# The ramp of a fused attention and MLP kernel: the linear matrix's products one visit sooner, one reciprocal one visit later

## The chip, the cores and the metric

The kernel runs on one core of a Trainium2 chip. The metric is the device time of one execution in microseconds (us), as the median of a few runs. Engines are named as in the profile: PE (TensorE matmul), PEld (its weight load), DVE (VectorE), ACT (ScalarE), POOL (GpSimd), SP (SyncE, which issues the DMAs).

## The reference

The inputs are `x` (4 x 12480 x 128), 32 inducing points, and the weights of an MLP with 2048 hidden units. Two attention blocks come first, then the MLP with a leaky activation whose slope `alpha` differs for each hidden unit.

```python
def mab(q, kv):
    s = scale * (q @ kv.transpose(0, 2, 1))
    s = s - s.max(-1, keepdims=True)
    a = np.exp(s)
    a /= a.sum(-1, keepdims=True) + 1e-09
    return a @ kv
h = mab(I, x)                   # 32 rows for each of the 4 batches
x = mab(x, h).reshape(49920, 128)
h = x @ w_in
g = np.maximum(h, 0.0) + alpha * np.minimum(h, 0.0)
out = (g @ w_out).astype(np.float32)
```

## The kernel before

The leaky activation is split: `g = (1 - alpha) * relu(h) + alpha * h`. The first part needs the hidden units, with `w_out` scaled by `1 - alpha` (`W1`). The second part is linear, so it is one 128 x 128 matrix, `Amat`, the product of `w_in` and `w_out` scaled by `alpha` (`winT` and `AW`, 16 products of 128 x 128 added up). The rows `a` of the second attention have 32 weights each, and both uses of them go through the 32 rows `h`: `HW` is `h` times `w_in`, `HA` is `h` times `Amat`.

**Visits.** The rows of a batch are cut into groups of 16 tiles of 128 rows, a group into blocks of 4 tiles. A block takes 4 visits. A visit issues four products `hh` = `a` times `HW` (L808; they share PE, 32 rows each), four activations of 128 x 512 from PSUM into `gt` (L821 on ACT or L823 on DVE), and then the 16 products of the visit before into the block's sum `bp` (L834). So the group of rows with number (0, 0) takes visits 0 to 3, 4 to 7, 8 to 11 and 12 to 15, and the second rows, group (0, 1), begin at visit 16. The linear products `bp` += `a` times `HA` (L861) are made for two blocks at a time; the first such pair waits until visit 8, and block 0 is finished there.

**The order is written by hand.** The engines run the program in the order in which it is issued. `at(n, fn, ...)` puts a small step behind the products of visit n; steps of one visit run in the order in which they were put there. Steps of the ramp that matter here:

- POOL scales `w_out` (L977 for `W1`, L986 for `AW`), then takes the maximum off the second rows' scores (L726), sums the first rows' exponentials (`first_sum`, ending in L1154), sums the second rows' (`b_sum`, ending in L736), and multiplies the second rows by their reciprocal (`b_mul`, L757).
- `linear_product`: the 16 products into a bank of PSUM (L996) and the cast to `Amat` on DVE (L999).
- `a_lin`: four small products `Amat` times `hT` (L619) and the cast to `HA` on DVE (L621).
- `first_rec`: the first rows' reciprocal on DVE (L1167), which waits for POOL's first sum. The output of the first four blocks is multiplied by it (L880).
- `b_rec`: the second rows' reciprocal on DVE (L749), which waits for POOL's second sum. `b_mul` waits for it, and `b_turn` has SP issue the transpose of the product (L766), which visit 16 reads.
- The four casts of a part of the next batch's `x` on ACT (L347) in visits 4 to 6.

**The planner.** `Plan.choose` searches once, before anything is issued, over all visits. It knows the costs given with `at` (`"s"` a PE step with a bank of PSUM, `"v"` DVE, `"a"` ACT, in ns) and chooses for each visit which activations go to ACT and which to DVE, which of the 8 PSUM banks each product uses, and whether the DVE or ACT part of a step is done at once or put off until between the second and the third activation of the next visit (`plan.then`, `run_waiting`). A chain with `("!", 0)` is not put off. The planner has no times for POOL and for DMAs.

Of the kernel before, what the change touches and what calls it, by code (L numbers as in the profile page):

```python
# [30 lines left out]
def kernel(  # L31
# [254 lines left out]
    def new_state(b):  # L286
        st = State()
        st.b = b
        st.pieces = whole_pieces if b else first_pieces
        st.np = len(st.pieces)  # L290
        st.xT = xt_pool.tile([C, NT, P], bf16, name="xT", tag="xT")
        st.xn, st.xs, st.s1, st.e1T, st.e1, st.s1p, st.hp = {}, {}, {}, {}, {}, {}, {}
        st.e2, st.m2, st.den2, st.rc, st.rep = {}, {}, {}, {}, {}

        st.mx = sm_pool.tile([P, NX], f32, name="mx", tag="mx")
        st.rm = sm_pool.tile([P, NX], f32, name="rm", tag="rm")
        st.fac = sm_pool.tile([P, NX], f32, name="fac", tag="fac")
        st.da = sm_pool.tile([P, NX], f32, name="da", tag="da")
        st.ex = sm_pool.tile([P, NX], f32, name="ex", tag="ex")
        st.den = sm_pool.tile([P, 1], f32, name="den", tag="den")  # L300
        st.hs = h_pool.tile([P, C], f32, name="hs", tag="hs")
        eng = nc.gpsimd if b else nc.vector
        eng.memset(st.mx[:], HIGH)
        eng.memset(st.da[:], 0.0)
        return st
# [380 lines left out]
    def b_exp(e, n):  # L686
        def work():
            nc.scalar.activation(out=e[:, :n], in_=e[:, :n], func=EXP, scale=scale)  # L688

        plan.then(work)  # L690
# [219 lines left out]
    st = new_state(0)  # L910
# [286 lines left out]
    def at(n, fn, *args, cost=()):  # L1197


        todo.setdefault(max(n, 0), []).append((fn, args, cost))  # L1200
# [5 lines left out]
    at(2, first_rest_exp, H, H, cost=[("a", 560), ("!", 0)])  # L1206
    at(2, first_turn_dma)
    at(6, first_rec, cost=[("v", 160)])
    at(6, linear_product, cost=[("s", 900), ("v", 210), ("!", 0)])
    at(7, a_lin, st, cost=[("s", 260), ("v", 210)])  # L1210
    blocks[0].later = True

    def on(b, fn, *args):
# [2 lines left out]
    for b, s, nt in groups[1:]:  # L1216
        n = first[b, s]
        when = [n - 23, n - 19, n - 16, n - 14, n - 13, n - 11, n - 9, n - 6]
        if (b, s) == (0, 1):
            when = [1, 2, 3, 4, 5, 7, 8, 8]  # L1220
        if (b, s) == (0, 2):
            when[7] = n - 7
        at(when[0], on, b, b_scores, s, nt, cost=[("s", 25 * nt), ("f", 0)])
        at(when[1], on, b, b_max, s, nt, cost=[("v", 70 + 33 * nt)])
        at(when[2], on, b, b_less_pool, s, nt)
        at(
            when[3],
            lambda b=b, s=s, nt=nt: b_exp(states[b].e2[s], nt),
            cost=[("a", 100 + 27 * nt)],
        )  # L1230
        at(when[4], on, b, b_sum, s, nt)
        at(when[5], on, b, b_rec, s, nt, cost=[("v", 160)])
        at(when[6], on, b, b_mul, s, nt)
        at(when[7], on, b, b_turn, s, 0, nt)
# [13 lines left out]
    for b in range(B - 1):  # L1248
# [3 lines left out]
        for p, pc in enumerate(whole_pieces):  # L1252
# [16 lines left out]
            else:  # L1269
# [9 lines left out]
                cost=[("s", 215 if f else 85), ("v", 800 if f else 460)],  # L1279
# [19 lines left out]
    for n, (blk, i) in enumerate(visits):  # L1299
# [9 lines left out]
        cost = nt * Plan.FREE if both else 0  # L1309
# [55 lines left out]
```

## Time and profile before

| | |
|---|---|
| median of 3 runs | 594.98 us (593.67 to 595.17) |
| profiled execution | 593.7 us, its span 591.9 us |
| granted TensorE clock | 0.998 |
| PE, PEld | 99%, 75% of the span |
| DVE, ACT, POOL | 90%, 91%, 37% |
| chain that ended last | PE 91%, DMA 5%, POOL 2% |

The span runs from the first to the last instruction; the rest of an execution's time lies around it. Busy time of PE includes the time in which a product that has been taken up waits. A timeline line gives start and length in us, the engine, the line of the kernel, the operation, what is written from what, shapes and count; in brackets is the idle time of the engine before it and what ended it. Lines of SPq are DMA issues.

### The profile page before, as it was taken

What the parts mean: (1) busy time and instruction counts of PE and PEld (TensorE: products, weight loads), DVE (VectorE), ACT (ScalarE), POOL (GpSimd) and SP (SyncE); (2) the same over time, 40 slices, a digit from 0 to 9 for tenths busy, and PEclk for the clock granted to TensorE, in tenths of its full rate; (3) what the DMA queues carried; (4) which work ended last, traced back from release to release, by engine and by line L of the source; (5) the groups of instructions that cost most, each with busy time, mean ns of one, the idle gap of its engine ahead of it and who ended that gap; (6) DMA issues with size and microseconds to landing.
All of it is one profiled execution on the core that took longest, in us unless ns stands there. A gap on an engine that the chain in (4) does not pass through costs nothing.

```text
span 591.9 us, 23144 instructions
## 1 busy us (share of the span) xinstructions
PE 584.5 (99%) x9500; PEld 441.3 (75%) x9500; DVE 535.5 (90%) x978; ACT 537.3 (91%) x1086; POOL 216.6 (37%) x260
## 2 busy tenths in 40 slices
PE   9999999999999999999999999999999999999997
PEld 6667777777777777777777777777777777777776
DVE  5889999999999898999999899999999999989996
ACT  5698999999999999999999999999999998999986
POOL 3494633323326426313226256124034034144010
PEclk9999999999999999999999999999999999999999
DMA  8969999233187999631368999731321331532421
GB/s 338 265 180 167 250 207 225 62 90 91 38 237 161 209 193 211 127 82 60 86 151 180 190 249 207 144 100 38 92 72 55 92 75 53 119 81 61 91 69 47
DMA packets 122347, 80.56 MB, mean 136 GB/s; under 512 B 103760, under 2 KB 106112, under 8 KB 119168
## 3 DMA queue, kind: packets, MB, share of 16 engines
q1 hardware_dynamic: 122016, 78.99, 56.3%
q8 instruction: 74, 1.21, 0.9%
q14 instruction: 33, 0.27, 0.2%
q10 hardware_dynamic: 224, 0.09, 0.1%
HBM read 28.07 MB, written 25.56 MB: 91 GB/s over the span
## 4 chain that ended last, share of the span: by engine, by line
PE 91%; DMA 5%; POOL 2%; DVE 0%; issue 0%; DVEq 0%; SPq 0%; ACT 0%; POOLq 0%
PE bp L834 64%; PE hh L808 21%; DMA xs<-in_x_dram 3%; PE bp L861 2%; DMA w_out_f<-in_moe_w_out_dram 2%; PE hh L644 2%; PE hh L473 1%; PE hh L379 1%; DMA e<-e1T 1%; POOL W L977 1%; POOL AW L986 1%; POOL t L712 0%; DVE gt L823 0%; DVEq L1360 0%; DVE xn L349 0%
## 5 line engine op out<-in xcount | busy, mean ns | idle before, releaser
L821 ACT ACTIVATE gt<-hh 128x512 bf16<-128x512 f32 x854 | 454.8, 605 | 36.0 <-PE hh L808 30.9
L823 DVE TENSOR_SCALAR gt<-hh 128x512 bf16<-128x512 f32 x706 | 453.5, 684 | 23.8 <-PE hh L808 13.3
L834 PE MATMUL bp<-W,gt 128*128 128x128 bf16 x6240 | 417.3, 220 | 0.2 <-DVE gt L823 0.2
L834 PEld LDWEIGHTS <-gt 128*128 128x128 bf16 x6240 | 349.4, 98 | 84.9 <-issue 76.6
L808 PE MATMUL hh<-a,HW 32*128 32x512 bf16 (+2 forms) x1664 | 156.2, 371 | 0.5 <-ACT gt L821 0.5
L757 POOL TENSOR_TENSOR rep<-e,rc 128x2048 bf16<-128x2048 f32 (+1 forms) x24 | 84.5, 3520 | 23.9 <-DVE rc L749 23.5
L726 POOL TENSOR_TENSOR e<-e,smx 128x512 f32<-128x512 f32 (+1 forms) x24 | 24.6, 1025 | 156.4 <-ACT gt L821 89.6
L808 PEld LDWEIGHTS <-HW 32*128 32x128 bf16 x1664 | 40.6, 91 | 41.7 <-issue 5.6
L712 POOL TENSOR_TENSOR t<-e 128x256 f32<-128x256 f32 (+1 forms) x24 | 17.2, 717 | 139.8 <-ACT e L688 139.7
L887 ACT COPY ob<-bp 128x512 f32<-128x512 f32 (+1 forms) x62 | 36.3, 585 | 4.3 <-PE bp L834 1.4
L712 POOL TENSOR_TENSOR t<-t 128x128 f32<-128x128 f32 (+3 forms) x100 | 30.3, 303 | 7.8
L330 POOL CAST xn<-xs 128x2048 bf16<-128x2048 f32 x17 | 32.1, 1888 | 2.8 <-DMA xs<-in_x_dram 2.3
L889 DVE COPY ob<-bp 128x512 f32<-128x512 f32 x32 | 22.0, 687 | 6.0 <-PE bp L834 6.0
L861 PEld LDWEIGHTS <-a 32*128 32x128 bf16 x392 | 15.0, 93 | 6.3 <-issue 0.5
L393 DVE TENSOR_SCALAR_CACHE_REDUCE s<-hh 128x512 f32<-128x512 f32 (+2 forms) x29 | 18.0, 619 | 1.6 <-PE hh L379 1.6
L861 PE MATMUL bp<-HA,a 32*128 32x128 bf16 x392 | 19.1, 214 | 0.2 <-DVE HA L621 0.2
L418 ACT ACTIVATE e1T<-s,rm 128x512 bf16<-128x512 f32 (+1 forms) x25 | 17.9, 718 | 0.6 <-DVE rm L402 0.6
L721 DVE TENSOR_REDUCE smx<-e 128x16 f32<-128x512 f32 (+1 forms) x24 | 15.9, 662 | 0.0
L963 PE MATMUL bp<-blank 128*128 128x256 bf16 x78 | 14.0, 316 | 1.2 <-DVE blank L909 1.2
L688 ACT ACTIVATE e<-e 128x512 f32<-128x512 f32 (+1 forms) x24 | 15.0, 625 | 0.2 <-POOL e L726 0.2
L489 DVE SCALAR_TENSOR_TENSOR hs<-hs,fac,hh 128x128 f32<-128x128 f32 (+1 forms) x25 | 8.6, 344 | 6.4 <-PE hh L473 5.7
L702 ACT COPY e<-hh 128x512 f32<-128x512 f32 (+1 forms) x23 | 13.9, 606 | 0.2
(110 smaller groups left out, 203.7 us busy)
## 6 DMA issues: line engine op xcount, KB each, us to landing
out_dram<-ob SPq DMA_DIRECT2D x97, 256.0 KB, 2.7
xs<-in_x_dram SPq DMA_DIRECT2D x23, 1024.0 KB, 6.6
xs<-in_x_dram SPq DMA_DIRECT2D x2, 512.0 KB, 9.1
w_in_f<-in_moe_w_in_dram SPq DMA_DIRECT2D x1, 1024.0 KB, 4.8
a<-rep SPq DMA_TRANSPOSE x25, 4.7
xT<-xn SPq DMA_TRANSPOSE x18, 6.0
e<-e1T SPq DMA_TRANSPOSE x18, 3.8
xs_left<-in_x_dram SPq DMA_DIRECT2D x4, 64.0 KB, 5.2
```

Source lines behind the costliest of these rows:

```text
L330: nc.gpsimd.tensor_copy(out=st.xn[s][:], in_=xs[:])
L393: nc.vector.tensor_scalar(out=s1[:parts, :cols], in0=ps[:parts, :cols], scalar1=-scale, scalar2=None, op0=MULT, op1=MIN, accum_out=st.mx[: ...
L712: nc.gpsimd.tensor_tensor(out=t[:, :n], in0=src[:, :n, :w], in1=src[:, :n, w : 2 * w], op=ADD)
L726: nc.gpsimd.tensor_tensor(out=st.e2[s][:, :n], in0=st.e2[s][:, :n], in1=st.m2[s][:, :n].unsqueeze(2).broadcast_to([P, n, M]), op=SUB,)
L757: nc.gpsimd.tensor_tensor(out=rep[:, :n], in0=st.e2[s][:, :n].unsqueeze(2).broadcast_to([P, n, R, M]), in1=rc[:, :n].unsqueeze(2).unsqueez ...
L808: nc.tensor.matmul(hh[:, q * cols + w.start : q * cols + w.stop], HWs[b][rows, v * P : (v + 1) * P], a2[rows, t0 : t0 + nt, :].rearrange(" ...
L821: nc.scalar.activation(out=gt[:, :cols], in_=hh[:, :cols], func=RELU)
L823: nc.vector.tensor_relu(gt[:, :cols], hh[:, :cols])
L834: nc.tensor.matmul(blk.acc[:, t * C : (t + 1) * C], gt[:, (q * nt + t) * P : (q * nt + t + 1) * P], W1[:, k, :], start=(not blk.begun), st ...
L861: nc.tensor.matmul(blk.acc[w, t * C : (t + 1) * C], blk.a2[rows, blk.t0 + t, w], HAs[b][rows, :], start=(not blk.begun and t == 0), stop=F ...
L887: nc.scalar.copy(out=ob[:, :nt], in_=acc)
L889: nc.vector.tensor_copy(out=ob[:, :nt], in_=acc)
```

## The change

The 16 products of the linear matrix go from visit 6 to visit 5 and the small products that follow from them from visit 7 to visit 6, each with the cast behind it. The second rows' reciprocal goes from visit 7 to visit 8, where the multiplication that reads it and the transpose stand already. `first_rec` stays in visit 6, now ahead of the small products instead of ahead of the 16. Costs are unchanged, but the planner sees them in other visits.

```diff
     at(6, first_rec, cost=[("v", 160)])
-    at(6, linear_product, cost=[("s", 900), ("v", 210), ("!", 0)])
-    at(7, a_lin, st, cost=[("s", 260), ("v", 210)])
+    at(5, linear_product, cost=[("s", 900), ("v", 210), ("!", 0)])
+    at(6, a_lin, st, cost=[("s", 260), ("v", 210)])
...
         if (b, s) == (0, 1):
-            when = [1, 2, 3, 4, 5, 7, 8, 8]
+            when = [1, 2, 3, 4, 5, 8, 8, 8]
```

The list `when` holds the visits of `b_scores`, `b_max`, `b_less_pool`, `b_exp`, `b_sum`, `b_rec`, `b_mul` and `b_turn`, in this order.

## The prediction

> **What bounds the kernel now.** I read the page first, then PE's timeline from 34 to 58 us, then the same stretch of DVE, POOL and SP, and last the chain of waits. The page:
>
> ```profile
> span 591.9 us, 23144 instructions
> PE 584.5 (99%) x9500; PEld 441.3 (75%) x9500; DVE 535.5 (90%) x978; ACT 537.3 (91%) x1086; POOL 216.6 (37%) x260
> ```
>
> PE is the bound, so an edit is worth what it takes out of PE's order, or puts into it. PE's timeline around the change (start, length, then engine and line; L808 are the four products that open a visit, L834 the sixteen that close the one before, L996 the linear matrix's products, L619 its small products, L861 the linear products that need HA):
>
> ```profile
> 38.53 0.40 PE L808 MATMUL hh<-a,HW 32*128 32x512 bf16 x4
> 39.76 1.06 PE L996 MATMUL hh<-AW,winT 128*128 128x128 bf16 x16
> 40.75 0.39 PE L808 MATMUL hh<-a,HW 32*128 32x512 bf16 x4
> 42.07 0.24 PE L619 MATMUL hh<-Amat,hT 128*32 128x128 bf16 x4
> 42.24 0.77 PE L808 MATMUL hh<-a,HW 32*128 32x512 bf16 x4
> 43.24 0.40 PE L861 MATMUL bp<-HA,a 32*128 32x128 bf16 x8 [0.22 <-DVE HA L621]
> 44.57 0.70 PE L808 MATMUL hh<-a,HW 32*128 32x512 bf16 x4
> 49.47 0.38 PE L861 MATMUL bp<-HA,a 32*128 32x128 bf16 x8
> ```
>
> Counting the L808 groups from 30.02 us, visits 5 to 9 begin at 37.20, 38.53, 40.75, 42.24 and 44.57, visit 12 at 49.24 and visit 16 at 54.77. A plain visit lasts 1.33 (37.20 to 38.53), and one with linear products 1.55 (visit 12: 49.24 to 50.79). Visit 6 lasts 2.22, which is 1.33 and 0.89 for sixteen products: no wait. Visit 7 lasts 1.49, which is 1.33 and 0.16 for four small ones: no wait. Visit 8 lasts 2.33 where 1.55 would do, so 0.78 is waiting. It has two parts: its L808 group takes 0.77 against 0.39, so 0.38 goes on PSUM banks; and L861 begins 1.00 after the visit's start, against 0.23 in visit 12, so 0.77 in all, of which 0.39 is left for HA. Visit 9's L808 group takes 0.70 against 0.39: 0.31 more on a bank. In all 1.08 us. The engine behind these waits is DVE:
>
> ```profile
> 41.40 0.25 DVE L1167 RECIPROCAL rec<-den 128x16 f32<-128x16 f32 x1 [0.49 <-POOL den L1154]
> 41.57 0.23 DVE L999 CAST Amat<-hh 128x128 bf16<-128x128 f32 x1
> 41.72 1.27 DVE L823 TENSOR_SCALAR gt<-hh 128x512 bf16<-128x512 f32 x2
> 42.91 0.28 DVE L621 CAST HA<-hh 128x128 bf16<-128x128 f32 x1
> 44.05 0.25 DVE L749 RECIPROCAL rc<-den 128x16 f32<-128x16 f32 x1 [0.86 <-POOL den L736]
> 44.22 0.63 DVE L823 TENSOR_SCALAR gt<-hh 128x512 bf16<-128x512 f32 x1
> ```
>
> Amat is cast only at 41.57, because the first rows' reciprocal (L1167) stands ahead of it and waits for POOL's sum; HA follows behind two activations and ends at 43.19. The second rows' reciprocal (L749) then holds DVE for 0.86, and visit 8's one activation on DVE stands behind it until 44.22; that one ends at 44.85, and PE's group of 44.57 waits for its bank. What feeds both:
>
> ```profile
> 33.03 4.03 POOL L986 TENSOR_TENSOR AW<-w_out_f,alT 128x512 bf16<-128x512 f32 x4
> 43.81 0.20 POOL L736 TENSOR_SCALAR den<-t 128x16 f32<-128x16 f32 x1
> 44.44 3.61 POOL L757 TENSOR_TENSOR rep<-e,rc 128x2048 bf16<-128x2048 f32 x1 [0.42 <-issue]
> 48.07 1.78 SPq L766 DMA_TRANSPOSE a<-rep  x1
> ```
>
> **The change, part by part.** No instruction is added or removed.
>
> Sixteen products, one visit sooner. On PE they move from 39.76 to the end of visit 5, where its L834 group ends 0.90 after 37.53, at 38.43. What they read is there: AW is written by 37.06 and winT landed near 30.7 (issue 25.40, 5.3 to landing). The cover is 1.4 us; if the loads of w_out came later by more than that, every further us would stand on PE. Their 0.89 leaves visit 6 and enters visit 5: visit 6 then begins at 39.42 and visit 7 at 39.42 + 1.33 + 0.16 = 40.91, the four small products having moved too; visit 8 begins at 42.24 as now. So the moves alone are worth nothing. Amat's cast (0.15 to the next start) goes ahead of visit 6's activations and of L1167; DVE is free there at about 39.0, and the sums come at about 39.6. Nobody else waits for it.
>
> HA. Its cast now comes from visit 6's work, right behind L1167, at about 41.6 or, if the planner puts it off, between visit 7's activations, at most 42.5. Visit 8 wants it at 42.47. So the 0.39 at L861 goes: **-0.39**. L1167 itself keeps its place and its POOL sum (41.37), so DVE still cannot pass 41.4 before it does visit 7's activations.
>
> Banks in visits 7 and 8. The 0.38 of visit 8 ends with visit 7's activations on DVE (41.72 and later) and ACT (41.51 and later, behind casts of x). Both are held as before. The small products' bank is now taken in visit 6, so one more is free in visit 8; against that, visit 6's activations start 0.89 later and visit 7 follows them 1.49 rather than 2.22 after. Best case -0.38 (all of it gone); worst a further wait as large as visit 9's, +0.31. I take **0**, the middle of two rows, because the same activations have to be done in the same time.
>
> The reciprocal, one visit later. L749 now stands behind visit 8's activations, so the one of 44.22 can run at about 43.2, and its bank is free well before visit 9: **-0.31**. POOL's sum still comes at 44.01, so if the reciprocal stands right behind that activation it runs at 44.05 as now. Queued behind it on DVE are visit 9's activations, which are not ready before 44.4 anyway (0.40 after the L808 start). If DVE takes the two output multiplications first (L880, 44.76 for two, 1.27), the reciprocal comes 1.2 later. Behind it waits the whole line of the second rows: POOL's multiplication of 3.61, SP's transpose, 4.3 from issue to landing by the DMA view, and visit 16. On POOL the casts of x (L335, L330) and on SP their transposes would shift by the same 1.2. Now the rows land at 52.4 and are read at 54.77: 2.4 us of cover. With visit 16 sooner by 0.7 and the landing later by 1.2, 0.5 is left. Cost: 0; bounds 0 and the rival's price below.
>
> Sum: -0.39 + 0 - 0.31 = -0.70 us. PE is the bound to the end, so it reaches the end. The profiled execution of before took 593.7 with a span of 591.9, 1.8 around it; I expect a span of 591.2 and 593.0 for such an execution. The median of the three runs, 594.98, lies 1.28 above the profiled one; taken off it, the forecast is **594.3**.
>
> The idle column alone shows only 0.22 of this, because waiting L808 groups are booked as busy; by idle time the edit would give 0.2 and not 0.7. I take the spacing of starts, since a visit's length is what the end feels. [...]
>
> **The rivals.** *The wait only changes its owner.* ACT works from 38.95 to 44.57 without a gap, on an exponential, four casts of x and activations. If PE comes sooner, ACT's activations end last instead, and visits 8 and 9 keep most of their waits; only L861's idle 0.22 is won: 594.8. For it: ACT's full timeline and visit 8's last L808, which waits for an ACT activation. Against: DVE loses 1.35 of idle time (0.49 and 0.86), which is two activations.
>
> *The second rows come late: slower.* The place is L808 of visit 16. If the reciprocal stands behind both output multiplications (45.3), POOL ends at 48.9 and SP issues at 49.3; the transposes' landings in this trace go from 3.1 to 6.2 us, so the rows arrive at 52.4 to 55.5. Visit 16 comes at 54.1 (54.77 - 0.70). It decides from an issue-to-landing of 4.8 on, and at 6.2 costs 1.4: 595.7; if visit 9's activations behind the late reciprocal lose the 0.31 again, 596.0. Against: 4.3 was this transpose's own time, which would leave visit 16 without a wait.
>
> *The planner decides otherwise for the rest.* It searches once over all visits, so other costs in visits 5 to 8 can move activations between ACT and DVE and change banks anywhere. Waits of PE after 46 us, by the same reading of starts, sum to about 3 us; a shuffle could win or lose some 2: 593.0 to 597.0. Against: in the second and third batch the same waits return 138.08 us apart (an L834 group of 1.24 at 195.86 and at 333.94, followed each time by an L808 group of 0.47), so the planner falls back into one pattern.
>
> *The change does nothing*, if the planner puts off Amat or HA as far as before: 595.0. Amat cannot be put off by its cost list, so this is weak.
>
> **How the numbers follow.** 0.3% is 1.8 us, about what a measurement of this kernel can tell from no change. Chances: forecast 0.56; other owner 0.15; late rows 0.13; planner 0.14; nothing 0.02. Faster by over 0.3% (below 593.2): 0.02 from the planner and 0.02 from a full -1.08 met by the runs' spread (1.3 below the median to 0.2 above), 0.04. Slower (above 596.8): 0.05 from the planner, 0.02 from rows landing later than any here, 0.03 from the runs' spread, 0.10. Within: 0.86. Range: the best sum is 593.9, and half of the lower spread takes it to 593.2; upward it takes in the late rows (596.0) and the nearer half of the planner's case, to 596.2.
>
> **What would show it.** L996 at about 38.4, HA before 42.5, visit 8's L861 0.2 to 0.6 after its first L808 and not 1.0, visit 9's L808 group at 0.40, visit 9 beginning near 44.2 and visit 10 near 45.9, no wait at visit 16, and the rest of PE's order as before. Wrong if visit 8 still takes over 2.1, if L749 starts after 45, or if the waits of later visits differ by more than 1 us.

## The result

The change made the kernel slower: 597.02 us median of 8 runs (594.75 to 599.22) against 593.62 of 8 runs before (592.79 to 595.17), ratio 1.0055, 95% interval [1.004, 1.007]. The forecast was 594.3, a gain. The profiled execution took 596.9 us with a span of 595.1, 3.2 more than the span of before. The page of the changed kernel, with the row of the opening products of a visit, and below it that row of the kernel before:

```profile
span 595.1 us, 23143 instructions
...
PE 584.9 (98%) x9500; PEld 441.4 (74%) x9500; DVE 536.5 (90%) x979; ACT 537.3 (90%) x1085; POOL 216.7 (36%) x260
...
L808 PE MATMUL hh<-a,HW 32*128 32x512 bf16 (+2 forms) x1664 | 156.0, 371 | 3.3 <-DMA a<-rep 2.8
```

```profile
L808 PE MATMUL hh<-a,HW 32*128 32x512 bf16 (+2 forms) x1664 | 156.2, 371 | 0.5 <-ACT gt L821 0.5
```

The engines' work is the same to within 1.0 us (DVE has 536.5 for 535.5). What is new is in the last column: PE stood idle for 2.8 us in front of one L808 group, for a transpose of the rows `a`.

**The ramp did what was forecast.** PE's timeline of the changed kernel in the lines that answer to those of before:

```profile
38.80 1.06 PE L996 MATMUL hh<-AW,winT 128*128 128x128 bf16 x16
39.79 0.40 PE L808 MATMUL hh<-a,HW 32*128 32x512 bf16 x4
...
41.28 0.59 PE L808 MATMUL hh<-a,HW 32*128 32x512 bf16 x4
...
42.80 0.39 PE L808 MATMUL hh<-a,HW 32*128 32x512 bf16 x4
43.03 0.38 PE L861 MATMUL bp<-HA,a 32*128 32x128 bf16 x8
...
44.35 0.39 PE L808 MATMUL hh<-a,HW 32*128 32x512 bf16 x4
```

Visit 0 began 0.37 later in this execution (30.39 against 30.02), before anything that the edit moves. Visit 8 lasts 1.55 (42.80 to 44.35), without a wait: L861 begins 0.23 after it. Visit 9's group takes 0.39. Only visit 7 has a wait of 0.20 on a bank. From visit 0 to visit 16 PE needs 23.85 us, 0.89 less than before.

**The loss sits at one place, visit 32,** where the third rows, group (0, 2), are first read. PE there in the kernel before, then in the changed kernel, and below it the changed kernel's clock by stretches (us, PE busy, PEld, DVE, ACT, POOL, granted clock, DMA share, GB/s):

```profile
78.39 0.40 PE L808 MATMUL hh<-a,HW 32*128 32x512 bf16 x4
...
79.73 0.40 PE L808 MATMUL hh<-a,HW 32*128 32x512 bf16 x4
...
81.18 0.53 PE L808 MATMUL hh<-a,HW 32*128 32x512 bf16 x4
```

```profile
76.86 1.07 PE L834 MATMUL bp<-W,gt 128*128 128x128 bf16 x16
80.73 0.61 PE L808 MATMUL hh<-a,HW 32*128 32x512 bf16 x4 [2.80 <-DMA a<-rep]
81.28 1.89 PE L834 MATMUL bp<-W,gt 128*128 128x128 bf16 x16
83.09 0.61 PE L808 MATMUL hh<-a,HW 32*128 32x512 bf16 x4
83.64 1.15 PE L834 MATMUL bp<-W,gt 128*128 128x128 bf16 x16
```

```profile
78.00:80.00 2.00, 0.00 (x0) 0.00 (x0) 0.47 (x1) 0.59 (x2) 0.00 (x0) 1.00 1.33 91
80.00:82.00 2.00, 1.27 (x12) 0.84 (x13) 0.56 (x1) 0.54 (x2) 0.00 (x0) 0.61 0.97 276
82.00:84.00 2.00, 2.00 (x20) 1.37 (x19) 1.49 (x4) 0.96 (x4) 0.00 (x0) 0.54 0.92 313
84.00:86.00 2.00, 2.00 (x33) 1.50 (x31) 1.91 (x4) 2.00 (x5) 0.00 (x0) 1.00 1.23 260
```

Visit 32 was due at 77.87 (visit 31's start and 1.33) and began at 80.73. Behind the wait the granted clock is 0.61 and 0.54, the sixteen products take 1.89 instead of 1.07, and visits 32 and 33 together 4.00 instead of 2.79. The balance: +0.37 for the later start, -0.89 from the ramp, +2.87 for the wait, +1.21 for the clock, 3.56 in all at visit 34. The spans differ by 3.2; the rest is won back far later, 0.24 near 230 us and 0.09 near 524.

**How the rows came to be late.** DVE's lines in the changed kernel, then SP's issues of before, then those of the changed kernel:

```profile
41.55 0.28 DVE L621 CAST HA<-hh 128x128 bf16<-128x128 f32 x1
...
43.29 1.29 DVE L823 TENSOR_SCALAR gt<-hh 128x512 bf16<-128x512 f32 x2 [0.16 <-PE hh L808]
44.50 0.24 DVE L749 RECIPROCAL rc<-den 128x16 f32<-128x16 f32 x1
```

```profile
49.95 1.56 SPq L894 DMA_DIRECT2D out_dram<-ob  x2
51.61 1.17 SPq L356 DMA_TRANSPOSE xT<-xn_left  x1
52.88 3.13 SPq L356 DMA_TRANSPOSE xT<-xn  x1
56.06 0.57 SPq L315 DMA_DIRECT2D xs<-in_x_dram  x1
...
69.38 1.19 SPq L449 DMA_TRANSPOSE e<-e1T_left  x1
...
72.93 2.31 SPq L766 DMA_TRANSPOSE a<-rep  x1
```

```profile
50.39 1.58 SPq L894 DMA_DIRECT2D out_dram<-ob  x2
52.06 2.10 SPq L356 DMA_TRANSPOSE xT<-xn_left  x1
54.26 3.26 SPq L356 DMA_TRANSPOSE xT<-xn  x1
57.57 1.00 SPq L315 DMA_DIRECT2D xs<-in_x_dram  x1
...
66.52 4.12 SPq L356 DMA_TRANSPOSE xT<-xn  x1
70.73 2.11 SPq L449 DMA_TRANSPOSE e<-e1T_left  x1
...
74.87 2.95 SPq L766 DMA_TRANSPOSE a<-rep  x1
```

The reciprocal runs 0.45 later, behind two activations (0.37 is the later start of this execution), and so do the second rows and the two output stores behind them (50.39 against 49.95). From there 0.44 grows to 1.51 at the load of x (57.57 against 56.06) and to 1.94 at the third rows' transpose. The first store lands 4.87 us after its issue (55.26) and not 2.96 (52.91). The load lands at 64.54 instead of 62.54, POOL's cast of it waits 1.64, and the third rows' multiplication starts at 66.45 instead of 65.39. But that multiplication is done at 70.06, and SP comes to the transpose of its rows only at 74.87. SP issues one thing after the other, and ahead of it the transpose of x at 66.52 takes 4.12 where it took 3.00, and the one of e at 70.73 takes 2.11 where it took 1.19. The rows land at 80.68. In the kernel before they landed at 78.30 and were read at 78.39: they had 0.09 us of cover, which is the time from a transfer's landing to its first reader.

### The profile page after: what moved, and what is told of

The parts are those of the page before. It is cut to its first block, busy times and chain, and to the rows that moved or that the text cites. A ratio compares the mean times of both kernels' runs of the same rounds, so it can differ in the third digit from the quotient of the medians.

```text
span 595.1 us, 23143 instructions
## 1 busy us (share of the span) xinstructions
PE 584.9 (98%) x9500; PEld 441.4 (74%) x9500; DVE 536.5 (90%) x979; ACT 537.3 (90%) x1085; POOL 216.7 (36%) x260
## 3 DMA queue, kind: packets, MB, share of 16 engines
q8 instruction: 74, 1.21, 0.9%
## 4 chain that ended last, share of the span: by engine, by line
PE 95%; DMA 4%; DVE 0%; DVEq 0%; ACT 0%; issue 0%; POOL 0%; SPq 0%
PE bp L834 65%; PE hh L808 22%; DMA xs<-in_x_dram 3%; PE bp L861 2%; PE hh L644 2%; PE hh L473 1%; DMA a<-rep 1%; PE hh L379 1%; PE bp L963 1%; PE hh L364 0%; PE hh L598 0%; PE hh L456 0%; DVEq L1360 0%; DVE xn L349 0%; PE hh L582 0%; PE hh L521 0%
## 5 line engine op out<-in xcount | busy, mean ns | idle before, releaser
L808 PE MATMUL hh<-a,HW 32*128 32x512 bf16 (+2 forms) x1664 | 156.0, 371 | 3.3 <-DMA a<-rep 2.8
L808 PEld LDWEIGHTS <-HW 32*128 32x128 bf16 x1664 | 40.3, 91 | 44.5 <-issue 5.8
L861 PEld LDWEIGHTS <-a 32*128 32x128 bf16 x392 | 15.0, 93 | 5.8
L861 PE MATMUL bp<-HA,a 32*128 32x128 bf16 x392 | 19.1, 214 | 0.0
```

The costliest lines, as they stand in the source:

```text
L808: nc.tensor.matmul(hh[:, q * cols + w.start : q * cols + w.stop], HWs[b][rows, v * P : (v + 1) * P], a2[rows, t0 : t0 + nt, :].rearrange(" ...
L861: nc.tensor.matmul(blk.acc[w, t * C : (t + 1) * C], blk.a2[rows, blk.t0 + t, w], HAs[b][rows, :], start=(not blk.begun and t == 0), stop=F ...
```

## The experiments

Every kernel was timed in 5 rounds beside the kernel before, unless said otherwise. The theories: A, the reciprocal's 0.45 us grows by itself along SP's queue; B, PE merely comes sooner to rows that had no cover; C, the transfers and not SP's order set when the rows land; F, formed after the first four, a packet of 16 KB of the queue that the DMA view lists as `q8 instruction` runs into the output stores.

**The two parts apart.** `e1_products`, against the changed kernel:

```diff
-            when = [1, 2, 3, 4, 5, 8, 8, 8]
+            when = [1, 2, 3, 4, 5, 7, 8, 8]
```

> The changed kernel with the second rows' reciprocal put back to visit 7; the 16 products and the small ones stay one visit sooner. On DVE this differs from the changed kernel in one place (the reciprocal stands two activations further ahead), PE's and SP's orders are the same. Theory A (the reciprocal's 0.45 us on POOL grows on SP's queue into 2.4 us at the third rows' transpose): POOL's multiplication starts at about 44.4 again, the third rows land at about 78.3, visit 32 comes at about 77.9 and waits 0.4, the clock stays full: 593 us, 0.5 below before. Rival B (PE comes 0.9 sooner to a transpose that had 0.1 us of cover, and the transfers' lateness is no matter of the reciprocal): landing near 80.7 and a wait of 2.8 as in the changed kernel, 597 us.

Measured: 594.21 us, ratio 1.0006 [0.9997, 1.0015]. The first store took 2.91, as before, and the third rows' transpose was issued at 72.80 (72.93 before). PE was due at visit 32 at 77.80 instead of 78.39, and the transpose landed at 78.87 instead of 78.30:

```profile
78.92 0.39 PE L808 MATMUL hh<-a,HW 32*128 32x512 bf16 x4 [1.05 <-DMA a<-rep]
```

The granted clock stayed at 1.00 from 74 to 86 us. So B holds for about half of this wait, 0.59; the other half, 0.57, is the transpose, which took 6.07 to land for 5.37. Together they take back more than the 0.48 that PE won from visit 0 to 16 (24.26). They do not make 3 us.

`e2_recip`, on the kernel before, has this diff the other way round: 7 becomes 8.

> The kernel before with the reciprocal alone moved from visit 7 to visit 8. On DVE it only changes places with one activation. If the reciprocal is the cause (A in its simple form): POOL's multiplication 0.4 later and the third rows landing 2 us late, 596 us or more. If it costs nothing by itself, since DVE waits for POOL's sum until 44.05 in both orders: multiplication at 44.4 as before, visit 9 sooner by 0.31, visit 32 waiting 0.2 for rows that land at 78.3: 593.4 us, within 0.3 of before. Rival B: as this, since PE comes only 0.3 sooner.

Measured: 593.58 us, ratio 0.9994 [0.9985, 1.0003]; the rows landed at 77.86, visit 32 did not wait. The reciprocal ran right when POOL's sum was there (43.80), as the prediction had it for the whole change; so this run has no late reciprocal, and does not test A. Neither part alone loses anything that can be told; the two together lose 0.55%.

**Where the chain can be broken.** `e3_turn` and `e4_load`, each against the changed kernel:

```diff
-            when[7] = n - 7
+            when[7] = n - 8
```

> The changed kernel with the transpose of the third rows (L766 of group (0, 2)) issued one visit sooner, which puts it on SP ahead of one transpose of e (L449) and one output store. A and B: issue at about 72.9 instead of 74.9, landing near 78.7, the wait at visit 32 falls from 2.8 to about 0.9, and the clock is not lowered after it: 3.3 us off, about 593.7 us. Rival C (the transfers, not SP's order, set the landing): landing at 80.7 as before, 597 us. If the transpose of e that is pushed back is needed at once, PE waits for it at L473 instead.

```diff
-                    0: (-1, -1, 7), 1: (-1, 9, 10), 2: (4, 9, 11), 3: (12, 20, 21)
+                    0: (-1, -1, 7), 1: (-1, 9, 10), 2: (4, 9, 11), 3: (7, 20, 21)
```

> The changed kernel with the load of the fourth piece of the next batch's x (1 MB, L315) issued in visit 7 instead of visit 12, so that it runs at about 47 to 51 us, where the DMA engines are nearly idle, and not from 57.6 to 64.5. Theory A (a queue of transfers and of SP's issues that is full from 50 to 80 us): POOL's cast of that piece no longer waits for it (1.6 us in the changed kernel), the third rows' multiplication starts at about 64.9 instead of 66.5, the issues behind it come 1 to 2 us sooner, and the wait at visit 32 is under 0.5: about 592.7 us, below before. Rival B: the wait stays near 2.8, 597 us. Against both: the second rows' transpose runs beside the load and lands up to 1 us later, which visit 16's cover of 1.4 takes.

`e3_turn`: 594.70 us, ratio 1.0011 [1.0002, 1.002], 1.0 more than expected. The stores landed late again (55.09), but the transpose was issued at 72.35, landed at 78.61, and visit 32 waited 1.17 idle, with a granted clock of 1.00 over the span. SP's order is part of the chain, and C is out. A is out too: the reciprocal ran at 44.05 here, to the hundredth as in the kernel before, and the stores were late all the same. `e4_load`: 593.83 us, ratio 1.0007 [0.9998, 1.0016]. No wait at visit 32, as A had it; but the load held up the second rows' transpose, which landed at 54.76 (52.78 in the changed kernel), and visit 16 waited 0.98. The cover that I had given as 1.4 was smaller than the load's price, a miss.

**The packet and the stores.** Each trace has 74 packets of 16 KB in `q8 instruction`, in the median some 256 PE instructions apart (matrix products and weight loads, about 19000 in all). Set beside the first output store (times in us; "packet after" counts from the store's issue; the last column is visits 32 and 33 together):

| kernel | store issued, landed | took | packet | packet after | third rows landed | wait at visit 32 | two visits |
|---|---|---|---|---|---|---|---|
| before | 49.95, 52.91 | 2.96 | 53.48 | 3.5 | 78.30 | 0 | 2.79 |
| e1_products | 49.34, 52.25 | 2.91 | 52.72 | 3.4 | 78.87 | 1.12 | 2.77 |
| e2_recip | 49.70, 52.66 | 2.96 | 53.09 | 3.4 | 77.86 | 0 | 2.79 |
| changed | 50.39, 55.26 | 4.87 | 52.28 | 1.9 | 80.68 | 2.87 | 4.00 |
| changed, again | 50.09, 55.13 | 5.04 | 51.83 | 1.7 | 80.24 | 2.79 | 4.19 |
| e3_turn | 49.95, 55.09 | 5.14 | 51.86 | 1.9 | 78.61 | 1.23 | 2.77 |
| e12_filler | 50.03, 55.08 | 5.05 | 51.79 | 1.8 | 80.51 | filled | 2.65 |
| e5_wide | 49.74, 52.73 | 2.99 | 53.76 | 4.0 | 78.12 | 0.95 | 2.77 |
| e11_narrow | 49.32, 54.08 | 4.76 | 51.22 | 1.9 | 79.45 | 1.68 | 2.77 |

Where the packet starts 1.7 to 1.9 after the store's issue, the store takes 4.8 to 5.1; where it starts 3.4 or more after it, 2.9 to 3.0. Of the five traces not in the table four fall in the same groups (`e6_products_turn` 3.4 and 2.92, `e9_all` 4.0 and 2.94, `e10_before_wide` 6.9 and 2.97, `e7_load6` 1.9 and 5.09). `e4_load` does not: 1.0 and 3.68. The second store of the pair, issued some 1.2 behind the first, narrows the step: with the packet 2.22 to 2.26 behind its issue it took 4.2 (`e1_products`, `e2_recip`, `e6_products_turn`), with 2.35 it took 2.66 (the kernel before). `e8_again` is the changed kernel unaltered, run once (596.59 us):

> The changed kernel once more, for a second profile. Theory F: where the packet of the instruction queue comes while the stores run (before 53), stores land after 55 and visit 32 waits 2 to 3; where it comes after them, visit 32 waits under 1 and the time is near 594.5. Theory A: the stores land after 55 each time.

The packet was early, the stores landed after 55, visit 32 waited 2.79. And here visit 0 began when it did in the kernel before (30.03), the reciprocal ran at 44.13, 0.08 later than there, and the first store was issued 0.14 later. SP came to the third rows' transpose 1.10 later (74.03), and it landed 1.94 later. So the 0.45 of the first profile was not needed for the loss.

The last two lines of the table change the number of PE instructions ahead of visit 0. `e5_wide`, against the changed kernel:

```diff
-    blank = const.tile([P, 2 * P], bf16, name="blank")
+    blank = const.tile([P, 4 * P], bf16, name="blank")
...
-            nc.tensor.matmul(ps[:, : 2 * P], blank[:, :P], blank[:], start=True, stop=True)
+            nc.tensor.matmul(ps[:, :w], blank[:, :P], blank[:, :w], start=True, stop=True)
...
-        for _ in range(n):
+        for w in [4 * P] * (n // 2) + [2 * P] * (n % 2):
```

> The changed kernel with the warm-up products on a blank tile twice as wide and half as many (512 columns instead of 256): the same PE time, but 64 PE instructions fewer before visit 0, so that each later 16 KB packet of the instruction queue, which come some 256 PE instructions apart in all traces so far, comes about 2.1 us later (64 at the 30 instructions a us of a visit). Theory F (in the changed kernel that packet, at 52.3, meets the two output stores of 50.4 and 51.6 on one DMA engine; the stores land 2.3 late, and SP's transposes and loads behind them pass it on to visit 32): packet near 54.4, the first store lands near 53.2, the third rows near 78.5, the wait at visit 32 under 1, about 593.3 us. Theory A in its first form (0.45 us of delay on POOL and SP grow by themselves): stores land at 55.3, third rows at 80.7, 597 us.

Measured: 594.80 us, ratio 1.0012 [1.0000, 1.0024], against 1.0055 of the changed kernel. The store was on time, the load landed at 62.33, the rows at 78.12, and the granted clock over the span was 1.00. What is left at visit 32 is the products' wait, 0.95. The time is 1.5 above what was expected; the profile has one more wait, 1.49 in the middle of an L861 group at 361.69, that it puts down to nothing it shows. The edit also brought the load of `w_out` and POOL's work behind it forward (POOL's second sum ended at 42.97, in `e8_again` at 43.51), but the reciprocal stands behind DVE's activations there and came only 0.28 sooner. The control, `e10_before_wide`, is this edit on the kernel before:

> The kernel before with the wider warm-up products alone, a control for e5_wide. Theory F: in the kernel before the packet of the instruction queue came after the first store had landed, so 64 instructions fewer gain nothing there: ratio 1.000, 594 us. If wider warm-up products are themselves worth some 2 us (a higher clock early, a shorter start), the time falls to 592.

593.46 us, ratio 0.9997 [0.9983, 1.001]: by itself the edit is worth nothing. `e11_narrow` goes the other way on `e1_products`, the first 17 warm-up products of 256 columns made as 34 of 128:

```diff
-    def warm(n):
+    def warm(n, w=2 * P):
...
-    warm(17)
+    warm(34, P)
```

> The kernel with the products sooner alone (e1_products, 594.2 us, in which the packet at 52.7 came after the first store had landed at 52.3), with the first 17 warm-up products of 256 columns made as 34 of 128: the same PE time, 34 PE instructions more, so the packet comes about 1.1 us sooner, near 51.5, while the stores issued at 49.4 and 50.5 run. Theory F: the stores land near 54.7, the third rows near 80 and visit 32 waits over 2, with a lowered clock behind it: 596.5 us, with the reciprocal unmoved. If the reciprocal's move is needed for the loss: 594.2.

594.82 us, ratio 1.0019 [1.0008, 1.003], 0.6 above `e1_products` (the two intervals overlap). The packet came where it was meant to, the store took 4.76 with the reciprocal unmoved, the wait rose from 1.12 to 1.68. So the first store can be late without the reciprocal's move, with 34 PE instructions more far ahead and the packet 1.9 behind its issue instead of 3.4. But the size was a quarter of what I had expected, and it did not come down the queue: the third rows' transpose was issued at 72.88, in `e1_products` at 72.80. Nearly all of the 0.56 lies between its issue and its landing, 6.57 for 6.07. Here the stores had been 0.8 sooner than in `e8_again` to begin with, and the load landed at 62.60, before POOL was free for it.

That leaves a rival that was not tried: later packets could meet the third rows' transpose itself. In the eight traces in which a packet starts 2.7 to 5.0 us after the issue of this transpose, it lands after 5.8 to 6.6 us; in the other six, after 4.7 to 5.6. `e5_wide` and `e11_narrow` change the number of PE instructions ahead of these packets too. So it is shown that PE instructions more or fewer far ahead shift the first packet against the store and the store's time with it (4.76 for 2.91 in `e11_narrow`, 2.99 for 4.87 in `e5_wide`), and in the changed kernel the rows' landing too (78.12 for 80.68, `e5_wide`); how much of the rows' lateness comes by the stores and SP's queue, and how much by later packets, is not.

**The clock.** `e12_filler`, on the changed kernel, has 12 products of 512 columns behind visit 31, read by nobody:

```diff
+    at(31, filler, cost=[("s", 2600)])
```

> The changed kernel with 12 products of 512 columns that nobody reads (2.56 us) at the end of visit 31, in the time in which PE waits for the third rows. If the wait of 2.8 is all of the loss, this costs nothing and gains nothing: 597 us. If PE's lowered clock behind the idle wait costs the 1.3 that visits 32 and 33 take too long: the clock stays full, these two visits take 1.4 each, and the time falls by 1.3 to 595.7 us, although PE does more.

595.65 us, ratio 1.0024 [1.0009, 1.0039], and the two visits took 2.65. PE and the clock:

```profile
77.36 2.75 PE L1216 MATMUL hh<-W,blank 128*128 128x512 bf16 x12
80.56 0.39 PE L808 MATMUL hh<-a,HW 32*128 32x512 bf16 x4 [0.45 <-DMA a<-rep]
80.88 1.07 PE L834 MATMUL bp<-W,gt 128*128 128x128 bf16 x16
```

```profile
80.00:82.00 2.00, 1.55 (x25) 1.10 (x24) 0.88 (x2) 0.96 (x2) 0.00 (x0) 1.00 0.79 242
82.00:84.00 2.00, 2.00 (x33) 1.46 (x30) 1.96 (x4) 2.00 (x6) 0.00 (x0) 1.00 0.92 337
```

The rows were as late as ever (80.51). 2.75 us of work without use made the kernel some 1.4 faster: the granted clock behind it is 1.00 and not 0.61 and 0.54, and the two visits take 2.65 and not 4.00.

**Versions.** `e6_products_turn` is `e1_products` with the line of `e3_turn`; `e7_load6` is `e4_load` with 6 for 7; `e9_all` is `e5_wide` with the line of `e3_turn`.

> The kernel with the products sooner and the reciprocal where it was (e1_products), with the third rows' transpose issued one visit sooner, ahead of one transpose of e. There the wait at visit 32 was 1.1, with issue at 72.8 and landing at 78.9. All theories that blame the landing: issue near 70.9, landing near 76.5, no wait at visit 32: 1.1 less than e1_products, 593.1 us and about 0.15% under before. If the products' gain is lost for another reason, 594.2 as e1_products.

593.22 us, ratio 0.9987 [0.9979, 0.9996]: the rows landed at 75.47, visit 32 began at 77.69 with no wait. It beats both kernels, by 0.13% the one before.

> The changed kernel with the load of the fourth piece of x in visit 6 instead of 12: issued at about 39.7, ahead of the first transpose of x, which has 10 us to spare, and not directly ahead of the second rows' transpose, which e4_load made 2.4 late (visit 16 waited 1.05). If the second rows land by 53.5 again: no wait at visit 16, third rows near 77 as in e4_load, no wait at visit 32: 592.8 us. If the two loads still stand in the way of the second rows, a wait of up to 1 at visit 16: 593.8 us.

593.22 us, ratio 0.9987 [0.9978, 0.9995], though in the profiled execution, the longest of the 12 (594.57), visit 32 waited 1.01 with the stores late; visit 16 did not wait.

> The changed kernel with the wider warm-up products (e5_wide) and the third rows' transpose one visit sooner (e3_turn). Theory F: the stores land near 53 as in e5_wide, the third rows' transpose is issued near 69.8 instead of 72.3 and lands near 75.6, visit 32 (77.2) does not wait: 0.95 less than e5_wide, about 593.5 us or 592.8 on a fast draw, under before. If the rows are late again: 594.8.

594.87 us, ratio 1.0023 [1.0005, 1.0041], a miss, with runs up to 599.9. Visit 32 was free, but further on, in the third batch, another group of the same kind now waited:

```profile
378.67 0.40 PE L808 MATMUL hh<-a,HW 32*128 32x512 bf16 x4 [0.97 <-DMA a<-rep]
```

This edit, too, has fewer PE instructions ahead of every later packet. That it is a packet which made these rows late was not tried.

## Why the prediction was wrong

- **The terms of the sum came out, in part by luck.** HA: -0.39 forecast; the wait is gone. Visit 9's bank: -0.31 forecast; gone. Banks of visits 7 and 8: 0 taken between -0.38 and +0.31; measured -0.18 (0.20 left in visit 7 for 0.38 in visit 8). In all -0.70 forecast, -0.89 measured. But the waits hang on when POOL's sums come, and the execution that I read had them late: the second sum ended 13.98 after visit 0 began, in the changed kernel 13.50, in `e2_recip` 13.36. `e2_recip`, where HA still comes late, needs 23.98 from visit 0 to 16; the products' move on top of it bought 0.13, not 0.57. The base was a draw as well: I took the median of three runs, 594.98, and eight gave 593.62, from which the same sum would make 592.9.
- **The step that failed is "PE is the bound to the end, so it reaches the end".** I laid the cover of the moved rows against visit 16 and stopped there. Visit 16 did keep its cover (landed 52.78, read 54.24). The next use of the same queue, visit 32, had 0.09 in the trace that I had before me, and by the forecast itself PE would come there 0.7 sooner: a wait of 0.6 and a gain of nearly nothing. `e1_products` shows that, with a slower transpose on top. The signs that I had named for the ramp all came; of the signs of being wrong the last came too, since a later visit's wait differs by more than 1 us.
- **"Cost: 0" for the reciprocal failed too, and not by a reciprocal later than forecast.** The planner gave DVE two activations of visit 8 ahead of it and not one, but in three of the four profiles that have the change and nothing else ahead of visit 16 it ran at 44.05 to 44.13, where the forecast had 44.05, and the stores and the rows were late in all four. Alone the move costs nothing (`e2_recip`); beside the products' move it costs 2.8 (597.02 against 594.21 in `e1_products`). With the products sooner PE comes sooner, and the packet came sooner too (51.8 to 52.3 for 53.48); the reciprocal keeps the stores from coming sooner with it (50.0 to 50.4 for 49.34 in `e1_products`). I had named what queues behind the reciprocal (POOL's casts, SP's transposes), but priced a delay of 1.2 at one reader only, and no meeting of transfers at all.
- **The rival of the late rows had the kind of loss, and the wrong place and reason.** It wanted a reciprocal behind both output multiplications, and was priced at visit 16, from 595.7 to 596.0. The reciprocal stood ahead of them; the rows that came late were the third, and the price was 2.87 and 1.21 for the clock. The trace before does not show the second: PE's longest idle stretch in it from 2 to 588 us is 1.05, with the granted clock at 1.00 behind it. The rival of an ACT wait did not come true, nor the planner's: behind the ramp the order of instructions on ACT, DVE, POOL and SP is that of before.
- **The clock.** In the changed kernel the granted clock is 0.50 from 80.44 to 83.85, and 1.00 in the stretches beside it. Idle stretches of 2.80 and 2.72 on PE were followed by longer visits in the two profiles of the changed kernel (4.00 and 4.19 for 2.79), those of up to 1.61 at visit 32 in no profile. Without the lowered clock the wait would have cost 2.87 and not 4.08 (an estimate: 2.87 and the 1.21 that visits 32 and 33 took longer).
- **Still open:** whether a packet and a store share a DMA engine, and why the packet jumps from 3.4 behind the first store to 1.9, cannot be read from these traces. That a packet holds up a store at all is my inference from the times, and `e4_load` does not fit it. Why SP's issues are longer 15 us behind a store that is 2 us late (4.12 for 3.00, 2.11 for 1.19) was not isolated either.

## What to carry to other kernels

Where PE is the bound, an earlier PE is worth what the least covered transfer of the whole program leaves of it (`e1_products` had won 0.48 by visit 16 and waited 1.12 at visit 32): lay the landing of every transfer against its reader, not only that of the one that is moved. Where one queue issues transposes, loads and stores in turn, a delay is not a constant along it (in `e8_again` it was 0.14 at a store and 1.10 at a transpose 24 us later); look for the point at which it grows (in the changed kernel behind the first store, from 0.44 to 1.51 at the load of x). If two edits each cost nothing (ratios 1.0006 and 0.9994), run them together (1.0055) before believing the sum.

## What the runs showed of the hardware

- The queue `q8 instruction` has 74 packets of 16 KB beside about 19000 instructions of PE, in the median some 256 apart. Where one started 1.7 to 1.9 us after the issue of the first 256 KB store, the store took 4.8 to 5.1 us to land, and where one started 3.4 or more after it, 2.9 to 3.0; `e4_load` (1.0 and 3.68) is in neither group. With 64 PE instructions fewer far ahead the packet started 4.0 after the store's issue for 1.9 (`e5_wide`), with 34 more 1.9 for 3.4 (`e11_narrow`).
- Behind idle waits of 2.80 and 2.72 us on PE two visits took 4.00 and 4.19 instead of 2.79, in the first at a granted clock of 0.50 for 3.41 us; with 12 products that nobody reads in the wait's place they took 2.65, at a clock of 1.00.
